# Fixed buffer places, a new order, x by token half and one scale per weight tile in a fused attention and MoE kernel

## The chip, the cores and the metric

One core of one Trainium2 chip runs the whole program; the other cores do nothing. The metric is the time of one execution on the device in microseconds, the median of several runs. Lower is better.

## What is computed

Three stages follow each other: a linear attention with decay in blocks of 64 rows, a gated layer without a nonlinearity, and a layer with a SoLU, a layer norm and an output projection.

```python
for b in range(nb):                       # q, k, v: (2, 8, 768, 64)
    intra = einsum('bhic,bhjc->bhij', qb, kb) * Dmask
    intra = einsum('bhij,bhjd->bhid', intra, vb)
    inter = einsum('bhid,bhde->bhie', qb * lam_pow, kv_state)
    out[:, :, sl] = intra + inter
    kv_state = lam_block * kv_state + einsum('bhsd,bhse->bhde', kb * rev_pow, vb)
x = out.transpose(0, 2, 1, 3).reshape(1536, 512)
x = ((x @ w_a) * (x @ w_b)) @ w_out       # 512 -> 1536 -> 512
h = x @ w_in                              # 512 -> 1024
solu = h * softmax(h)
ln = (solu - mean(solu)) / sqrt(var(solu) + 1e-6) * g_ln
return ln @ w_out2                        # 1024 -> 512
```

All inputs are float32.

## The kernel before

Every large product is done with numbers split into two float16 parts, high and low: `mm3` (line 142) issues three products for each one, high by high, high by low, low by high. The splitting is done on ScalarE (ACT, the high part), VectorE (DVE, the low part, by a SCALAR_TENSOR_TENSOR) and GpSimd (POOL). Before a split, a scale that is a power of two is found from the largest absolute value (`amax`, line 114, then `pow2`, line 128, which uses products on PE with the result `pm` to spread the value over the partitions).

The work is cut into 12 row tiles of 128 tokens for the attention (`n`), three token blocks of 512 (`t`), and weight tiles. Pieces of work are generators; each `next` issues one step. The letters in `ORDER` name them: G loads, A scores (`pss`, then `sc` on DVE), K and Q decays on POOL (`kd`, `qd`), C the attention's products (`px`) and their maximum `xst`, T the state (`pst`), X the scale of x (`sx`), Y its split (`xh`), J sums of x (`tt`, `xt`), D decodes a weight tile (`fab` and the like, and its maximum `st_ab`), p and P find the scale of weights (`sab`), S splits them (`wab`, `wo`, `wi`), H and E make sums of weights and split them (`s`, `ws`), L products of the gated layer in the plain way (`pa`, `pb`), R the same for a pair of weight tiles by seven instead of eight products with sums of halves (Strassen's way; `rA`, `rB`, `rC`, with `p` and `c` on ACT, DVE and POOL), M the projection back (`py`), U, V, B, F and the weight sums I, k the scale and the sums of y (`sy`, `yf`, `yu`, `yv`, `yt`), N the third layer's products (`hA`, `hB`, `hC`), n the SoLU and norm (`e`, `st`), Z the split and transposition of `e` (by DMA, and for the last two row tiles by PE: `pz`), W the output (`po`, `ob`).

`ORDER` is a long string of such words, written out. The engines run in the order in which it issues their instructions; nothing reorders them later. A word is one step, so the string is the whole schedule, for all engines and the DMA queue (SP) at once.

What the change and the prediction touch: tiles come from rotating pools, one each for `k` (41 buffers), `raw` (2), `row` (8), `state` (4) and the 8 PSUM banks (`bank`, line 103; `tile_of`, line 106), so a new tile takes the next buffer in turn. x is kept as two tiles by halves of the 512 model columns, each with all 512 tokens (`split_x`, line 290). Each row tile of 128 tokens has its own scale, two in one `sx` (line 286), and each weight tile has two, one for w_a and one for w_b, in `sab` (`scale_f`, `scale_w`, lines 358 and 361); so a split of a weight tile is two ACT and two DVE instructions of 512 or 256 columns (`split_w`, line 409; `split_s`, line 451). Products that compute nothing are issued by `warm` (line 182), with the identity as weights: 22 at the start, and by the table `FILL` 24 ahead of C 1, 36 ahead of T 5, 34 ahead of the scale X 3 and 18 ahead of C 8. `L1` (line 473) is the plain product, with 512 columns, except for block 0 and tile 0 (`HALVED`), where it is done by two halves of the tokens.

Of the kernel before, what the change touches and what calls it, by code (L numbers as in the profile page):

```python
# [86 lines left out]
PLAIN, PLAINW = [0, 1, 2], [0, 1]  # L87

TOP = 12
BUFS = {"k": 41, "raw": 2, "row": 8}  # L90
# [825 lines left out]
```

## Time and profile before

| | us |
|---|---|
| runs (3): lowest, median, highest | 455.75, 456.03, 456.63 |
| profiled execution: span, from its first to its last instruction | 454.0 |
| PE busy | 441.3 |
| DVE busy | 337.8 |
| ACT busy | 248.7 |
| POOL busy | 233.1 |

The span is that of one execution under the hardware profiler, and the page gives no time of its own for it beyond the span. The timed runs include what lies around the span; their median is 2.0 us above it. Busy times of an engine are merged, so that instructions that overlap are not counted twice.

### The profile page before, as it was taken

What the parts mean: (1) busy time and instruction counts of PE and PEld (TensorE: products, weight loads), DVE (VectorE), ACT (ScalarE), POOL (GpSimd) and SP (SyncE); (2) the same over time, 40 slices, a digit from 0 to 9 for tenths busy, and PEclk for the clock granted to TensorE, in tenths of its full rate; (3) what the DMA queues carried; (4) which work ended last, traced back from release to release, by engine and by line L of the source; (5) the groups of instructions that cost most, each with busy time, mean ns of one, the idle gap of its engine ahead of it and who ended that gap; (6) DMA issues with size and microseconds to landing.
All of it is one profiled execution on the core that took longest, in us unless ns stands there. A gap on an engine that the chain in (4) does not pass through costs nothing.

```text
span 454.0 us, 8039 instructions
## 1 busy us (share of the span) xinstructions
PE 441.3 (97%) x3204; PEld 276.5 (61%) x3204; DVE 337.8 (74%) x571; ACT 248.7 (55%) x397; POOL 233.1 (51%) x259
## 2 busy tenths in 40 slices
...
GB/s 302 415 214 270 196 92 281 185 186 95 94 0 1 2 1 165 121 180 0 95 92 76 203 99 88 0 95 1 1 20 39 60 23 95 68 116 90 144 47 46
DMA packets 30373, 48.76 MB, mean 107 GB/s; under 512 B 22272, under 2 KB 22528, under 8 KB 27008
## 3 DMA queue, kind: packets, MB, share of 16 engines
...
q14 instruction: 12, 0.10, 0.1%
...
## 4 chain that ended last, share of the span: by engine, by line
PE 74%; DVE 6%; POOL 4%; DMA 2%; ACT 1%; issue 1%; ACTq 0%; DVEq 0%; POOLq 0%
PE py L145 21%; PE rA L145 14%; PE po L145 13%; PE rB L145 7%; PE hA L145 4%; PE rC L145 3%; PE pa L145 3%; PE pb L145 3%; PE hB L145 2%; DMA raw<-in_wab_dram 2%; PE hC L145 1%; DVE fab L353 1%; DVE tt L320 1%; DVE ws L459 1%; DMA zT<-zr 1%
## 5 line engine op out<-in xcount | busy, mean ns | idle before, releaser
L145 PE MATMUL py<-g,wo 128*128 128x512 f16 x432 | 94.4, 379 | 0.0
L145 PEld LDWEIGHTS <-wab 128*128 128x128 f16 x744 | 72.1, 98 | 36.0 <-issue 0.9
L145 PEld LDWEIGHTS <-wo 128*128 128x128 f16 x432 | 42.2, 98 | 50.4
L145 PE MATMUL po<-wo,zT 128*128 128x512 f16 (+1 forms) x312 | 63.5, 363 | 0.3 <-DMA zT<-zr 0.3
L145 PEld LDWEIGHTS <-ws 128*128 128x128 f16 x576 | 56.1, 98 | 7.6 <-DVE ws L459 0.5
L145 PEld LDWEIGHTS <-zT 128*128 128x128 f16 x312 | 30.5, 98 | 32.0 <-DMA zT<-zr 0.8
L563 POOL TENSOR_TENSOR g<-c,g 128x512 f16<-128x512 f32 x24 | 31.2, 1319 | 33.8 <-ACT g L561 33.7
L145 PE MATMUL rA<-xt,ws 128*128 128x256 f16 x288 | 35.2, 273 | 0.0
L496 POOL TENSOR_TENSOR g<-asb,g 128x512 f16<-128x512 f32 x12 | 16.0, 1338 | 34.1 <-ACT g L494 34.1
L145 PE MATMUL pa<-xh,wab 128*128 128x512 f16 (+1 forms) x156 | 33.3, 363 | 0.0
L145 PE MATMUL pb<-xh,wab 128*128 128x512 f16 (+1 forms) x156 | 33.2, 363 | 0.0
L519 ACT ACTIVATE p<-rA 128x512 f32<-128x512 f32 x36 | 21.2, 595 | 20.5 <-PE rA L145 20.5
L807 POOL TENSOR_TENSOR zr<-e,zr 128x512 f16<-128x512 f32 x20 | 24.7, 1256 | 10.1 <-ACT zr L803 10.1
L351 ACT ACTIVATE raw<-raw 128x1024 f32<-128x1024 f32 x26 | 29.4, 1140 | 0.0
L848 ACT ACTIVATE ob<-po,glm 128x512 f32<-128x512 f32 (+1 forms) x13 | 8.4, 654 | 34.4 <-PE po L145 28.6
L552 POOL TENSOR_TENSOR c<-p,p 128x512 f32<-128x512 f32 x12 | 15.7, 1311 | 20.6 <-ACT p L519 19.6
L145 PEld LDWEIGHTS <-yt 128*128 128x128 f16 x144 | 14.0, 98 | 16.8 <-DVE yt L651 0.3
L557 DVE SCALAR_TENSOR_TENSOR c<-c 128x512 f32<-128x512 f32 x24 | 20.2, 850 | 4.9 <-ACT c L554 4.6
L425 ACT ACTIVATE wab<-fab,sab 128x512 f16<-128x512 f32 (+1 forms) x24 | 14.4, 641 | 10.5 <-DVE sab L136 10.4
L353 DVE SCALAR_TENSOR_TENSOR fab<-raw,fab 128x1024 uint32<-128x1024 uint32 x12 | 15.5, 1289 | 6.3 <-ACT raw L351 6.3
L764 ACT ACTIVATE e<-h,st,ch 128x512 f32<-128x512 f32 (+1 forms) x12 | 12.3, 1022 | 14.1 <-DVE st L758 14.1
L428 DVE SCALAR_TENSOR_TENSOR wab<-fab,sab,wab 128x512 f16<-128x512 f32 (+1 forms) x24 | 18.9, 822 | 1.1 <-ACT wab L425 1.1
...
## 6 DMA issues: line engine op xcount, KB each, us to landing
...
zT<-zr SPq DMA_TRANSPOSE x20, 3.1
...
```

The lines of the kernel that those rows point to most:

```text
L145: nc.tensor.matmul(o, w[a], x[b], start=start and i == 0, stop=stop and i == 2, skip_group_check=True)
L351: nc.scalar.activation(hi.bitcast(F32), hi.bitcast(F32), AF.Prelu, scale=2.0 ** -112, alpha=2.0 ** 32)
L353: nc.vector.scalar_tensor_tensor(out=flat, in0=hi, scalar=3, in1=flat, op0=ALU.logical_shift_left, op1=ALU.bitwise_or)
L425: nc.scalar.activation(w[:, z, 0, c], src[:, z, c], AF.Copy, scale=ss[:, z:z + 1])
L428: nc.vector.scalar_tensor_tensor(out=w[:, z, 1, c], in0=src[:, z, c], scalar=ss[:, z:z + 1], in1=w[:, z, 0, c], op0=ALU.mult, op1=ALU.subt ...
L496: nc.gpsimd.tensor_sub(g[:, 1], a, g[:, 0])
L519: nc.scalar.activation(r, o, AF.Copy, scale=2.0 ** -28)
L552: nc.gpsimd.tensor_sub(c1[:, 1], p167, p5)
L557: nc.vector.scalar_tensor_tensor(out=c[:, :, 0], in0=c[:, :, 0], scalar=2.0, in1=c[:, :, 1], op0=ALU.mult, op1=ALU.mult)
L563: nc.gpsimd.tensor_sub(g[:, 1], c[:, :, 0], g[:, 0])
L764: nc.scalar.activation(e2[:, z], x, AF.Exp, bias=st[:, 2:3], scale=c, accum_out=st[:, 3 + k:4 + k])
L807: nc.gpsimd.tensor_sub(lo, e[z], hi)
```

## The change

Five things change. `SLOTS` names for each new tile which buffer it takes, and the pools of small tiles give each its own place. `ORDER` is another string. x is kept as two tiles by token half, each with all 512 columns: one ACT and one DVE instruction of 512 columns split a row tile, where there were two each of 256, and two row tiles share one scale. L reads the two token halves apart, so its products have 256 columns, and those of block 0 and tile 0 have 128. A weight tile has one scale for w_a and w_b: its split, and that of its sums, is one ACT and one DVE instruction of twice the columns. `FILL` is empty; the products that compute nothing now have a tile of ones as weights that DVE writes at the very start, and a new word `w` issues four of them, 12 times in `ORDER`.

```diff
-FILL = {('C', 1): 24, ('T', 5): 36, ('X', 3): 34, ('C', 8): 18}
+FILL = {}
...
-         "A,1 D,ab,0 A,1 K,1 K,1 C,1 D,ab,0 Q,2 A,2 C,1 G,ab,2 G,qk,6 K,2 G,kv,6 C,2 A,2 Q,3 A,2 A,3 D,ab,0 X,0 C,2 K,3 A,3 K,3 T,1 X,0 K,2 p,0 A,3 T,1 C,3 O,3 "
...
+ORDER = ("G,qk,0 G,qk,2 G,qk,1 G,kv,0 G,kv,1 G,qk,3 w,9 G,qk,5 w,7 w,6 G,ab,0 G,kv,2 A,0 G,kv,3 A,2 Q,2 A,0 A,0 G,qk,4 A,1 A,2 A,1 G,kv,5 C,0 K,0 A,1 K,0 C,0 "
...
-BUFS = {"k": 41, "raw": 2, "row": 8}
...
+    "raw": ("01010101010101011010011010"),
...
+    "state": ("012301302130201320"),
...
+    taken = {tag: iter(SLOTS.get(tag, "")) for tag in ("bank", "k", "raw", "row", "state")}
+
+    def slot(tag):
+        return tag + str(ABC.index(next(taken[tag], "0")))
 
     def bank(nm):
-        return ps.tile([P, W], F32, tag="bank", name=nm)
+        return ps.tile([P, W], F32, tag=slot("bank"), name=nm)
...
-        nc.vector.tensor_reduce(out=m, in_=pm[:, :n * P].rearrange("p (g c) -> p g c", g=n), axis=AX.X, op=ALU.max)
+        nc.vector.tensor_reduce(out=m, in_=pm[:, :n * P], axis=AX.X, op=ALU.max)
...
+    hot = const.tile([P, P], BF16, name="hot")
+    nc.vector.memset(hot, 1.0)
...
-            nc.tensor.matmul(o, identb, identb, start=True, stop=True, skip_group_check=True)
+            nc.tensor.matmul(o, hot, hot, start=True, stop=True, skip_group_check=True)
+
+    def heat(i):
+        warm(bank("heat")[:, :P], 4)
+        yield
...
-            xs[t] = [t_k("xh", (P, 2, 2, W), F16) for _ in range(2)]
-        s = sx[n // 2][:, 0, n % 2:n % 2 + 1]
+            xs[t] = [t_k("xh", (P, KD, 2, W // 2), F16) for _ in range(2)]
+        s = sx[n // 2][:, 0]
...
-        for h in hs:
-            nc.scalar.activation(xs[t][h][:, :, 0, c], o[:, 2 * h:2 * h + 2], AF.Copy, scale=s)
-        yield
-        for h in hs:
-            xh, xl = (xs[t][h][:, :, z, c] for z in range(2))
-            nc.vector.scalar_tensor_tensor(out=xl, in0=o[:, 2 * h:2 * h + 2], scalar=s, in1=xh, op0=ALU.mult, op1=ALU.subtract)
+        xh, xl = (xs[t][j % 2][:, :, z, j // 2 * P:(j // 2 + 1) * P] for z in range(2))
+        nc.scalar.activation(xh, o, AF.Copy, scale=s)
+        yield
+        nc.vector.scalar_tensor_tensor(out=xl, in0=o, scalar=s, in1=xh, op0=ALU.mult, op1=ALU.subtract)
         yield
...
-        return pow2(stab[:, f // 2, f % 2], 2, sab[:, :, f], TOP)
+        return pow2(stab[:, f:f + 1], 1, sab[:, :, f:f + 1], TOP)
...
+    def both(hi, lo, src, s):
+
+        nc.scalar.activation(hi, src, AF.Copy, scale=s)
+        yield
+        nc.vector.scalar_tensor_tensor(out=lo, in0=src, scalar=s, in1=hi, op0=ALU.mult, op1=ALU.subtract)
         yield
...
+        if nm == "ab":
+            at = f if f // 2 in PLAINW else f - f % 2
+            c = slice(W // 2 if f % 2 and f // 2 not in PLAINW else 0, W)
+            yield from both(w[:, :, 0, c], w[:, :, 1, c], src[:, :, c], sab[:, 0, at:at + 1])
+            return
...
-        ss = sab[:, 0, 2 * p]
-        for z in range(2):
-            nc.scalar.activation(w[:, z, 0], src[:, z], AF.Copy, scale=ss[:, z:z + 1])
-            yield
...
+        yield from both(w[:, :, 0], w[:, :, 1], src, sab[:, 0, 2 * p:2 * p + 1])
...
-                    xk = x[kk // 2][:, kk % 2]
-                    mm3(rows(pp[z]), (w[:, 0, ks], w[:, 1, ks]), (rows(xk[:, 0]), rows(xk[:, 1])), kk == 0, kk == KD - 1)
+                    for q in range(2):
+                        xk = x[q][:, kk].rearrange("p z (i c) -> p z i c", i=2)[:, :, i]
+                        mm3(rows(pp[z])[:, q], (w[:, 0, ks], w[:, 1, ks]), (xk[:, 0], xk[:, 1]), q == 0 and kk == 0, q == 1 and kk == KD - 1)
```

The order on DVE at the start of the program, behind the decay masks. Before:

```order
L232 TENSOR_TENSOR sc<-pss,mask 128x512 x2
L115 TENSOR_REDUCE xst<-px 128x1
L232 TENSOR_TENSOR sc<-pss,mask 128x512 x2
L353 SCALAR_TENSOR_TENSOR fab<-raw,fab 128x1024
L115 TENSOR_REDUCE xst<-px 128x1
L232 TENSOR_TENSOR sc<-pss,mask 128x512 x2
```

With the change:

```order
L251 TENSOR_TENSOR sc<-pss,mask 128x512 x5
L128 TENSOR_REDUCE xst_221<-px 128x1 x2
L251 TENSOR_TENSOR sc<-pss,mask 128x512 x2
L146 TENSOR_REDUCE pm<-pm 128x1
L148 TENSOR_SCALAR pm<-pm 128x1
L149 TENSOR_SCALAR sx_256<-pm 128x1
```

The scores of two and a half row tiles come ahead of the first maximum of x, and the first scale of x ahead of the first decoded weight tile.

The order on DVE at the end of the program. `e` and `st` are the norm's tiles of the last two row tiles, `zT` their transposed parts. Before:

```order
L775 SCALAR_TENSOR_TENSOR e<-e,st,hA 128x512
L775 SCALAR_TENSOR_TENSOR e<-e,st,h_4633 128x512
L792 TENSOR_SCALAR e<-e,st 128x1024
L778 BN_STATS bn<-e 128x6 x2
L780 BN_AGGR st<-bn 128x2
L792 TENSOR_SCALAR e<-e,st 128x512 x2
L827 TENSOR_TENSOR zT<-pz,zT 128x4x128 x4
```

With the change:

```order
L794 BN_STATS bn_4877<-e 128x6 x2
L796 BN_AGGR st_4820<-bn_4877 128x2
L794 BN_STATS bn_4841<-e 128x6 x2
L808 TENSOR_SCALAR e<-e,st_4820 128x512
L796 BN_AGGR st_4825<-bn_4841 128x2
L808 TENSOR_SCALAR e<-e,st_4820 128x512
L808 TENSOR_SCALAR e<-e,st_4825 128x1024
L841 TENSOR_TENSOR zT<-pz,zT 128x4x128 x4
```

The row tile whose half lies in PSUM is now finished first, the other one (1024 columns) last, and the low parts of `zT` for both stand behind that.

On PE the transposes of the two row tiles stand together with the change, ahead of the first half of the last output tile:

```order
L158 LDWEIGHTS zT
L158 MATMUL po<-wo_3856,zT 128x512
L834 MATMUL pz<-ident,e 128x128 x16
L158 LDWEIGHTS zT
L158 MATMUL po<-wo_3647,zT 128x256
```

Before they were two groups of 8 with a whole output tile between them and one behind the second.

## Rows read from the trace of the kernel before

**Rows 1.** The page's busy times: share of the span, number of instructions.
```profile
PE 441.3 (97%) x3204; PEld 276.5 (61%) x3204; DVE 337.8 (74%) x571; ACT 248.7 (55%) x397; POOL 233.1 (51%) x259
```
**Rows 2.** Windows: stretch, length, then busy PE, PEld, DVE, ACT, POOL, clock, DMA share.
```profile
0.00:6.79 6.79, 4.61 (x38) 4.05 (x38) 3.08 (x9) 1.49 (x2) 3.94 (x16) 1.00 0.67 230
6.79:15.00 8.21, 7.91 (x104) 6.85 (x104) 4.94 (x7) 2.57 (x3) 3.77 (x6) 1.00 1.02 411
15.00:58.33 43.33, 37.43 (x598) 32.88 (x598) 37.79 (x80) 23.55 (x41) 33.29 (x38) 1.00 0.63 252
58.33:102.20 43.87, 43.19 (x282) 22.66 (x279) 40.41 (x62) 26.20 (x41) 24.89 (x19) 1.00 0.53 193
102.20:440.00 337.80, 337.50 (x2114) 203.07 (x2115) 250.29 (x415) 192.12 (x307) 167.20 (x184) 1.00 0.24 70
...
60.07:450.71 390.64, 390.09 (x2451) 231.84 (x2450) 290.25 (x475) 220.60 (x350) 190.64 (x200) 1.00 0.27 84
```
**Rows 3.** The chain of waits that ended last: start, us, what.
```profile
50.91 2.06 PE pm L184 x34
...
57.55 0.78 DVE xh L304 x2
...
60.07 2.69 PE pa L145 x12
...
66.38 1.02 PE px L249 x16
...
102.81 1.31 PE rA L145 x12
...
450.71 0.47 ACT ob L848
```
**Rows 4.** DVE's instructions by line and form: count, busy us, mean ns, idle before.
```profile
L428 DVE SCALAR_TENSOR_TENSOR wab<-fab,sab,wab 128x512 f16<-128x512 f32 x16 | 13.9, 904 | 1.1 <-ACT wab L425 1.1
L459 DVE SCALAR_TENSOR_TENSOR ws<-s,sab,ws 128x512 f16<-128x512 f32 x16 | 13.9, 917 | 0.0
L304 DVE SCALAR_TENSOR_TENSOR xh<-px,sx,xh 128x256 f16<-128x256 f32 x24 | 10.3, 475 | 1.1 <-ACT xh L300 0.9
L115 DVE TENSOR_REDUCE xst<-px 128x1 f32<-128x512 f32 x12 | 8.1, 685 | 3.9 <-PE px L249 3.9
L418 DVE SCALAR_TENSOR_TENSOR wo<-fo,s,wo 128x1024 f16<-128x1024 f32 x4 | 6.7, 1725 | 0.0
L679 DVE SCALAR_TENSOR_TENSOR wsi<-si,wsi 128x1024 f16<-128x1024 f32 x4 | 4.9, 1271 | 0.0
L775 DVE SCALAR_TENSOR_TENSOR e<-e,st,hA 128x512 f32<-128x512 f32 x6 | 4.5, 745 | 0.2
```
**Rows 5.** Timeline of the start: start, us, instructions, idle before and what ended it.
```profile
1.64 2.53 PE L184 MATMUL warm<-identb 128*128 128x128 bf16 x22 [1.64 <-DVE identb L179]
...
4.68 2.08 PE L227 MATMUL pss<-qk 64*128 64x128 f32 x16 [0.52 <-DMA qk<-in_qk_dram]
...
10.21 1.16 PE L227 MATMUL pss<-qk 64*128 64x128 f32 x16
```
**Rows 6.** Timeline around the scale of y for block 1.
```profile
299.10 0.22 PE L125 MATMUL pm<-identb,ry 128*128 128x128 bf16 x1
...
306.64 1.23 DVE L651 TENSOR_TENSOR yt<-yu,yt 128x1024 f16<-128x1024 f32 x1 [0.74 <-ACT yt L649]
```
**Rows 7.** Timeline of the end.
```profile
417.63 15.70 PE L145 MATMUL po<-wo,zT 128*128 128x512 f16 x72
...
431.93 1.00 DVE L792 TENSOR_SCALAR e<-e,st 128x512 f32<-128x512 f32 x2 [2.06 <-POOL st L789]
...
433.17 1.04 PE L820 MATMUL pz<-ident,e 128*128 128x128 f32 x8
```
**Rows 8.** DVE by line and form in 58.4:102.2 alone.
```profile
L459 DVE SCALAR_TENSOR_TENSOR ws<-s,sab,ws 128x512 f16<-128x512 f32 x3 | 4.9, 1679 | 0.0
...
L115 DVE TENSOR_REDUCE xst<-px 128x1 f32<-128x512 f32 x2 | 1.4, 692 | 0.6 <-PE px L249 0.6
```

More of the change, by code (lines that the diff above doesn't have):

```diff
@@ L89 @@
 TOP = 12
-BUFS = {"k": 41, "raw": 2, "row": 8}
+ABC = "0123456789abcdefghijklmnopqrstuvwxyzABCDEFGHIJKLMNOPQRSTUVWXYZ"
+SLOTS = {
+    "bank": ("01234567012345601475106140567056527053607563404761437653464636320621367013706123723076745367352137014670734161746713406225741236603623322603"
+          "0366143575102602364122012107635241064371206453"),
+    "k": ("0123456789abcdefghijklmnopqrstuvwxyzABCDE123ad4756cg98bkenphfmsoAtDqC2luBz3moy1bv9ebsuE60t24uzCs4581s41gAhgA60b51Evrflc01D6fDqB632qy7gD3yz8u"
+          "3y4zAnyuCdwapjixpjd29ouagwDismBeq06ktcwDjBfh6lpDfopjxfa3s0jprvyAafhn047bEksxCpmvl815zBjDAa6nrh04y"),
+    "raw": ("01010101010101011010011010"),
+    "row": ("012345671204576310241653025376134176704171701451047362264670232437402420232403701204127351246041652734102635407162342536720431256"),
+    "state": ("012301302130201320"),
+}
 @with_exitstack
@@ L251, in products @@
         if n // 2 not in xst:
-            xst[n // 2] = sm.tile([P, 2], F32, name="xst")
+            xst[n // 2] = sm.tile([P, 2], F32, name=f"xst{n // 2}")
         amax(xst[n // 2][:, n % 2:n % 2 + 1], o)
@@ L257, in fade @@
         b, c = order[n]
-        olds[n] = sl.tile([P, NP, D], F32, tag="state", name="old", bufs=4)
+        olds[n] = t_state("old", (P, NP, D))
         nc.gpsimd.tensor_mul(olds[n], state[n - B], dec[:, :, P - 1:P].to_broadcast([P, NP, D]))
@@ L271, in carry @@
         yield
-        new = sl.tile([P, NP, D], F32, tag="state", name="state", bufs=4)
+        new = t_state("state", (P, NP, D))
         if c == 0:
@@ L286, in scale_x @@
     def scale_x(m):
-        sx[m] = const.tile([P, 2, 2], F32, name=f"sx{m}")
-        return pow2(xst[m], 2, sx[m], TOP, FILL.get(("X", m), 0))
+        sx[m] = const.tile([P, 2, 1], F32, name=f"sx{m}")
+        yield from pow2(xst[m], 2, sx[m], TOP, FILL.get(("X", m), 0))
     def split_x(n):
@@ L334, in body @@
     wst = {nm: const.tile([P, m, 2], F32, name=f"st_{nm}") for nm, m in size.items() if nm != "ab"}
[L336 removed]
+    stab = const.tile([P, KA], F32, name="st_ab")
     fw, wt, scl = {}, {}, {}
[L339 removed]
+    sab = const.tile([P, 2, KA], F32, name="sab")
     def decode(nm, f):
         raw = raws.pop((nm, f))
[L344 removed]
+        hi = raw.rearrange("p z n w -> p (z n) w")[:, :, 1]
+        low = raw.rearrange("p z n w -> p (z n w)").bitcast(U16)[:, 1::4]
         x = fw[nm, f] = t_k("f" + nm, (P, 2, W))
         flat = x.rearrange("p z n -> p (z n)").bitcast(U32)
[L347 removed]
+        nc.scalar.activation(flat, low, AF.Copy, bias=-0.49994, scale=2.0 ** -13)
         yield
[L350 removed]
         nc.scalar.activation(hi.bitcast(F32), hi.bitcast(F32), AF.Prelu, scale=2.0 ** -112, alpha=2.0 ** 32)
@@ L371, in scale_w @@
             nc.vector.tensor_mul(st, st, gl)
-        r = sm.tile([P, 1], F32, name="r1")
+        r = sm.tile([P, 1], F32, name=f"r1{nm}")
         amax(r, st)
@@ L388, in scale_w @@
             k = 2 * len(PLAINW)
-            both = sab[:, 0, k:].rearrange("p (f e) z -> p f e z", e=2)
-            nc.vector.tensor_copy(both[:, :, 1], both[:, :, 0])
+            pairs = sab[:, 0, k:].rearrange("p (f e) -> p f e", e=2)
+            nc.vector.tensor_copy(pairs[:, :, 1], pairs[:, :, 0])
             turn(sab)
@@ L400, in scale_w @@
         yield
-    def halve(f, s, t):
-        nc.scalar.activation(t[:, 0, :], f, AF.Copy, scale=s)
+    def both(hi, lo, src, s):
+        nc.scalar.activation(hi, src, AF.Copy, scale=s)
         yield
-        nc.vector.scalar_tensor_tensor(out=t[:, 1, :], in0=f, scalar=s, in1=t[:, 0, :], op0=ALU.mult, op1=ALU.subtract)
+        nc.vector.scalar_tensor_tensor(out=lo, in0=src, scalar=s, in1=hi, op0=ALU.mult, op1=ALU.subtract)
         yield
@@ L415, in split_w @@
             s = scl["ro"][:, 2 * f:2 * f + 1] if nm == "o" else scl[nm][:, 0]
-            nc.scalar.activation(w[:, :, 0], src, AF.Copy, scale=s)
-            yield
-            nc.vector.scalar_tensor_tensor(out=w[:, :, 1], in0=src, scalar=s, in1=w[:, :, 0], op0=ALU.mult, op1=ALU.subtract)
-            yield
+            yield from both(w[:, :, 0], w[:, :, 1], src, s)
             return
-        ss = sab[:, 0, f if f // 2 in PLAINW else f - f % 2] if nm == "ab" else (scl["ro"] if nm == "o" else scl["glm"])[:, 2 * f:2 * f + 2]
-        c = slice(W // 2 if nm == "ab" and f % 2 and f // 2 not in PLAINW else 0, W)
+        if nm == "ab":
+            at = f if f // 2 in PLAINW else f - f % 2
+            c = slice(W // 2 if f % 2 and f // 2 not in PLAINW else 0, W)
+            yield from both(w[:, :, 0, c], w[:, :, 1, c], src[:, :, c], sab[:, 0, at:at + 1])
+            return
+        ss = (scl["ro"] if nm == "o" else scl["glm"])[:, 2 * f:2 * f + 2]
         for z in range(2):
-            nc.scalar.activation(w[:, z, 0, c], src[:, z, c], AF.Copy, scale=ss[:, z:z + 1])
+            nc.scalar.activation(w[:, z, 0], src[:, z], AF.Copy, scale=ss[:, z:z + 1])
             yield
         for z in range(2):
-            nc.vector.scalar_tensor_tensor(out=w[:, z, 1, c], in0=src[:, z, c], scalar=ss[:, z:z + 1], in1=w[:, z, 0, c], op0=ALU.mult, op1=ALU.subtract)
+            nc.vector.scalar_tensor_tensor(out=w[:, z, 1], in0=src[:, z], scalar=ss[:, z:z + 1], in1=w[:, z, 0], op0=ALU.mult, op1=ALU.subtract)
             yield
@@ L453, in split_s @@
         w = wt["s", p, k] = t_k("ws", (P, 2, 2, W), F16)
-        ss = sab[:, 0, 2 * p]
-        for z in range(2):
-            nc.scalar.activation(w[:, z, 0], src[:, z], AF.Copy, scale=ss[:, z:z + 1])
-            yield
-        for z in range(2):
-            nc.vector.scalar_tensor_tensor(out=w[:, z, 1], in0=src[:, z], scalar=ss[:, z:z + 1], in1=w[:, z, 0], op0=ALU.mult, op1=ALU.subtract)
-            yield
+        yield from both(w[:, :, 0], w[:, :, 1], src, sab[:, 0, 2 * p:2 * p + 1])
     gs = {t: {} for t in range(NB)}
@@ L505, in R1, with product @@
         u, v = (lambda z, k=k: wt["s", p, k][:, z] for k in range(2))
-        def product(o, w, k, x, i, start, stop):
+        def product(o, w, k, x, start, stop):
             for z in range(2):
@@ L511, in product, with part, sums @@
                     ks = slice((2 * k + kk) * P, (2 * k + kk + 1) * P)
-                    mm3(o[:, z], (w(z)[:, 0, ks], w(z)[:, 1, ks]), (x[:, kk, 0, i * H:(i + 1) * H], x[:, kk, 1, i * H:(i + 1) * H]), start and z == 0 and kk == 0, stop and z == 1 and kk == 1)
+                    mm3(o[:, z], (w(z)[:, 0, ks], w(z)[:, 1, ks]), (x[:, kk, 0], x[:, kk, 1]), start and z == 0 and kk == 0, stop and z == 1 and kk == 1)
+        def part(k, i):
+            return x[i][:, 2 * k:2 * k + 2]
+        def sums(k, i):
+            return xt[t][k][..., i * H:(i + 1) * H]
         def acc(nm):
@@ L522, in R1 @@
         A, Bk = acc("rA"), acc("rB")
-        product(A, f, 0, x[0], 0, True, False)
+        product(A, f, 0, part(0, 0), True, False)
         yield
-        product(Bk, u, 0, xt[t][0], 0, True, False)
+        product(Bk, u, 0, sums(0, 0), True, False)
         yield
@@ L528, in R1 @@
         yield
-        product(A, u, 1, xt[t][0], 1, False, False)
+        product(A, u, 1, sums(0, 1), False, False)
         yield
@@ L532, in R1 @@
         yield
-        product(Bk, v, 1, x[1], 1, False, True)
+        product(Bk, v, 1, part(1, 1), False, True)
         yield
@@ L536, in R1 @@
         yield
-        product(A, v, 0, xt[t][1], 0, False, False)
+        product(A, v, 0, sums(1, 0), False, False)
         yield
@@ L542, in R1 @@
         C = acc("rC")
-        product(C, f, 1, x[1], 0, True, True)
+        product(C, f, 1, part(1, 0), True, True)
         yield
@@ L546, in R1 @@
         yield
-        product(A, h, 1, xt[t][1], 1, False, True)
+        product(A, h, 1, sums(1, 1), False, True)
         yield
@@ L570, in L2 @@
         if t not in yst:
-            yst[t] = sm.tile([P, KD], F32, name="ym")
+            yst[t] = sm.tile([P, KD], F32, name=f"ym{t}")
         o = pys[t, d] = bank(f"py{d}")
@@ L582, in scale_y @@
     def scale_y(t):
-        r = sm.tile([P, 1], F32, name="ry")
+        r = sm.tile([P, 1], F32, name=f"ry{t}")
         amax(r, yst[t])
@@ L591, in scale_y @@
             turn(sx[m])
-        c = sm.tile([P, 1], F32, name="c")
+        c = sm.tile([P, 1], F32, name=f"c{t}")
         nc.vector.tensor_scalar(c, s[:, 1], scl["oi"], None, op0=ALU.mult)
-        for j in range(NJ):
-            n = t * NJ + j
-            ch = scl["ch", t, j] = const.tile([P, 2], F32, name=f"ch{t}{j}")
-            ix = sx[n // 2][:, 1, n % 2:n % 2 + 1]
+        for i in range(NJ // 2):
+            ch = scl["ch", t, i] = const.tile([P, 2], F32, name=f"ch{t}{i}")
+            ix = sx[2 * t + i][:, 1]
             nc.vector.scalar_tensor_tensor(out=ch[:, 0:1], in0=ix, scalar=ix, in1=c, op0=ALU.mult, op1=ALU.mult)
@@ L734, in L3 @@
         product(A, y[1], at[1], si(3), False, True)
+        hs[t, 2 * i + 1] = [A]
         yield
@@ L740, in L3 @@
         nc.gpsimd.tensor_sub(r, p167, p5)
-        hs[t, 2 * i + 1] = (A, r)
+        hs[t, 2 * i + 1].append(r)
         yield
     def norm(t, j):
-        ch = scl["ch", t, j]
+        ch = scl["ch", t, j // 2]
         c, cn = ch[:, 0:1], ch[:, 1:2]
-        st = sm.tile([P, 16], F32, name="st")
+        st = sm.tile([P, 16], F32, name=f"st{t}{j}")
         h = hs[t, j]
```

45 lines of the change are left out of this document (18 added, 27 removed), and 98 rows, old and new, of the table ORDER.

## Prediction

> **What bounds the kernel now.** I read the page's busy times first: PE is busy 97% of the span [rows 1], so time can only come out of PE's work or its 12.7 us of idle. The windows, by stage, tell where that idle lies [rows 2]: from the start of L1(1,0) at 60.07 to the last product at 450.71 PE is busy 390.09 of 390.64 us. Before 60.07 it is busy 51.2 us (441.3 - 390.1), so 8.9 us are idle, and the last 3.29 us are the output's tail. The kernel has two stages: a first one in which PE waits for something, and a second in which PE runs without a break.
>
> What the first stage waits for: the chain goes from DVE to PE and back until `xh` of row tile 7 ends at 58.33 [rows 3]; with it and a few products L1(1,0) can start. DVE is busy 3.08 + 4.94 + 37.79 = 45.8 us of these 58.33 [rows 2], and idle 12.5: 3.7 us until its first `sc`, 3.3 until 15 us while the DMA engines run at a share of 1.02, 5.5 after that. So DVE, and early on the loads, set when L1(1,0) starts; PE sets the rest. PE does fill this stage with 112 products that compute nothing.
>
> **PE's own work.** A 128-column product costs 2.06/34 = 60.6 ns, a 256-column one 1.31/12 = 109.2, a 512-column one 2.59/12 = 215.8 [rows 3]. Removed: 112 fillers, -6.8 us. Added: 12 `heat` steps of 4, +2.9. L1 reads x in two halves: 264 products of 512 columns become 528 of 256 (+0.7), and the 48 of L1(0,0) become 96 of 128 columns (+0.6). The single scale for w_a and w_b drops 4 products of `pm`, -0.4. Sum -3.0 us. All fillers stand ahead of L1(1,0), where PE waits anyway, so they pay nothing by themselves. Behind that point the order moves one C step (2.04 us) forward and one T step (0.6) back, L1's halves cost +0.7 and two `pm` leave: **-1.0 us**.
>
> **Start of L1(1,0).** I count what DVE does before it, by the order, with rows for each [rows 4]. Before: 17 `sc`, 8 maxima, 3 decodes and 2 maxima of `fab`, 16 `tt`, 16 halves of `xh`, 2 of `wab` and small ones, 46.9 us by the rows; it was busy 42.7 without the mask, a ratio of 0.91, since neighbours overlap. After: 20 `sc`, 4 decodes, 8 `tt`, and `xh` as 8 pieces of 512 at 0.745 (the row with a PSUM input) in place of 16 at 0.475: 45.1, times 0.91 = 41.1 us. So -1.6 us of work.
>
> DVE's idle I set at 7.7 us against 12.5. Until the first `sc` 3.2: the warm-up products no longer wait 1.64 us for `identb` [rows 5], but qk still lands near 4.7, so only half of that comes through, PE being faster for the first scores (2.08 us cold, 1.16 later [rows 5]). Until 15 us 2.0: qk 0, 2 and 1 come first and the order has five `sc` in a row, where before DVE stood until `px`. After that 2.5: it has `sc` and `tt` to do where it waited for the x scale. The ends are 6 and 12.5 (nothing gained). DVE is then done at 41.1 + 3.1 + 7.7 = 51.9. PE has 43.6 us of work before L1(1,0), mostly from 4.7 us on, so it can be there by about 50. I take 53.0 for 60.07: **-7.1 us**; the ends are -9 and -2.9.
>
> **The R stretch.** Here the order asks more of DVE. Between `xh` of tile 7 and L1(2,1), which now comes early and needs `xh` of tile 11, DVE has 7 + 3 decodes, 8 maxima of `fab`, 16 `tt`, 6 wide and 2 half `wab`, 5 wide `ws`, 7 products of L1, and small ones. A wide `wab` or `ws` of 1024 takes the place of two of 512 (0.904 and 0.917). No row shows it: the nearest are `wsi` 1.271 and `wo` 1.725 [rows 4]; I take 1.57, since two halves lose one fixed part of about 0.24 (2 x 0.904 - 1.57). By rows that is 73.2 us, and in 58.33:102.20 DVE was busy 40.4 for 41.4 by rows, 0.976 [rows 2]: 71.4. With 1.5 us of idle DVE is ready at 51.9 + 71.4 + 1.5 = 124.8. PE has 69.0 us of products between L1(1,0) and L1(2,1), so it is there at 122.0. PE waits **+2.8 us**, spread over the `ws` and `wab` it needs. The ends are 0 (1.271) and +9, worked out under the rivals. Before, PE had 0.7 us of idle in that stretch [rows 2].
>
> **Middle.** From U's `pm` to the second product of N(1,1) PE now has 9.0 us of other work; the chain through `yf`, `yu` and `yt` took 299.10 to 307.87 = 8.8 before [rows 6]. That is no margin: **+0.4 us**, ends 0 and 2. Other weights, `g` and `wo` are ready with over 6 us to spare by the sums of each engine's work, so they cost nothing as long as PE is not ahead of these sums by that much.
>
> **Tail.** Before, the last product of N(2,1) ended at 417.63, and its first transposes came at 433.2, the others one output tile later [rows 7]. Now both pairs stand together behind three output tiles, 3 x 5.2 = 15.5 us later. Behind N(2,1) DVE must do for both row tiles: two sums and three maxima, the exp's small steps, three products by the scale, four statistics, three last scalings, by the rows 12.7 us; it waits for two exps (1.7 and 0.9) and twice for POOL's 2 us of root (2.06 shown [rows 7], less what DVE does meanwhile: 2.6 together). That is 17.9 us. The first pair of transposes (0.9) is cover: 17.9 - 15.5 - 0.9 = 1.5, and 0.5 more as DVE is still at the tile before: **+2.0 us**, ends 0 and 4. In exchange no tile stands between; the last tile is unchanged.
>
> **Sum.** -7.1 - 1.0 + 2.8 + 0.4 + 2.0 = -2.9 us against the profiled execution's span of 454.0: 451.1. The median of the runs is 456.0, 2.0 above the span (launch and end); the same 2.0 on top gives **453.1 us**, 0.6% less.
>
> **Rivals.** 0.2% of this kernel is 0.9 us; a measurement can't tell less from no change, so "same" is 455.1 to 456.9.
>
> *The waits don't come (0.18).* If wide pieces cost 1.271 as `wsi` does, DVE needs 68.2 us and PE never waits in the R stretch; with a tail of +0.5 the sum is -7.1 - 1.0 + 0.5 = -7.6: 448.4 us. For it: DVE has idle in almost all of the second stage (250 of 337.8 us busy [rows 2]). Against it: `wo` at 1.725, four times.
>
> *DVE becomes the bound (0.20), the slower side.* POOL's sums of weights run beside `ws`, and there a 512-wide `ws` took 1.679 in place of 0.917 [rows 8]. If the wide one stretches in full, 3.36 us, for three of the five `ws` that PE needs, that is 3 x 1.79 = +5.4: 458.5. For all five it is +9.0: 462.1. It decides from +2.9, an average `ws` above 2.15 us, on. For it: before, DVE was already 92% busy there (40.4 of 43.9 us [rows 2]) and PE hardly waited. Against it: fewer and wider instructions also meet POOL less often.
> The Trainium skill (SBUF — State Buffer, Who interferes with whom) says that a DVE instruction with two SBUF inputs and a GpSimd instruction that reads SBUF shut each other out for a whole instruction. By that rule a wide `ws` waits once, not twice: 1.271 + (1.679 - 0.745) = 2.2 us as an estimate from the rows, +3.2 in all, and the time would be 456.3, no change. The trace agrees in that `ws` stretches beside POOL's sums and `xst`, with one input in PSUM, does not [rows 4, 8].
>
> *The early idle stays (0.10).* If the loads and not the order hold DVE back, L1(1,0) starts at 57.2 and the R stretch and the tail still cost 5.8: -2.9 - 1.0 + 5.8 = +1.9, 457.9. For it: the DMA share of 1.02.
>
> *PE falls back to its lower clock (0.06).* The first warm products took 115 ns each [rows 5], 128 columns at 1.2 GHz; the granted clock in the rows stays at 1.00. Without the fillers PE has some 6.7 us of work in the 11 us ahead of L1(0,0). If that costs the higher clock, L1(0,0) takes 11.7 us for 5.8, L1(1,0) starts near 59, and the later DVE wait is covered: -1.1 - 1.0 + 2.4 = +0.3, 456.3. The Trainium skill (TensorE: Matmul & The Clock Gate, HAM oscillation) says that idle gaps of PE bring the clock down. No row here shows a fall after the start.
>
> **How the numbers follow.** The forecast has 0.46, with a range of its own of 451 to 455.5: 0.43 of that is faster, 0.03 same. With the first rival faster is 0.61. Same is 0.03, the clock 0.06 and 0.04 from the mild form of the DVE rival: 0.13. The rest, 0.16 and 0.10, is slower: 0.26. The range reaches from 448.0, which holds the first rival, to 459.5, which holds the `ws` case with three of five; outside lie all five and both ends together.
>
> **What would show it.** Right: L1(1,0) starts near 53; between it and L1(2,1) PE shows waits of 1 to 5 us in sum, released by DVE `ws`, `wab` or `xh`; behind the third-last output tile PE waits 1 to 4 us for DVE's last scaling `e`; wide `ws` near 1.6. PE has 244 more products, busy about 3 us less in work. Wrong: L1(1,0) after 57, or waits of PE above 6 us in the R stretch, or waits in places that none of these steps names, such as a PSUM bank that an engine frees late, since every buffer now has a fixed place.

## Result and profile after

The changed kernel takes **444.52 us** (median of 4 runs, 444.46 to 444.59), the kernel before 455.89 beside it (455.04 to 456.63): a ratio of 0.9755, 95% interval 0.974 to 0.977. The forecast was 453.1 with a range of 448.0 to 459.5. The side was right, the size was not: 11.4 us came, not 2.9, and the time lies outside the range. In the profiled execution the span fell from 454.0 to 442.7.

The page's busy times after, to be read against [rows 1]:

```profile
PE 436.8 (99%) x3448; PEld 297.7 (67%) x3448; DVE 323.3 (73%) x524; ACT 241.0 (54%) x365; POOL 236.2 (53%) x259
```

PE has 4.5 us less work (441.3 to 436.8) and its idle time fell from 12.7 us to 5.9. The windows tell where; columns as in [rows 2]: stretch, length, busy PE, PEld, DVE, ACT, POOL, clock, DMA share. Cut at the start of L1(1,0), which moved from 60.07 [rows 3] to 49.42:

```profile
0.00:49.42 49.42, 47.57 (x753) 41.39 (x754) 42.67 (x84) 22.79 (x31) 33.13 (x53) 1.00 0.95 373
49.42:117.58 68.16, 68.08 (x683) 59.58 (x683) 65.92 (x98) 55.95 (x73) 41.73 (x30) 1.00 0.45 164
...
49.42:439.39 389.97, 389.20 (x2697) 256.29 (x2696) 280.62 (x441) 217.80 (x335) 203.09 (x207) 1.00 0.25 78
```

Nearly all of the gain, 10.65 of 11.3 us, lies ahead of L1(1,0). There the work of PE fell by 3.7 us (51.23 to 47.57) and its idle time by 7.0 (8.84 to 1.85). Behind that point the kernel is 0.65 us shorter (393.93 to 393.28). The chain of waits (start, us, what) is less one-sided: it runs over the loads and POOL until 20.85, over PE to 60.0, over DVE from there to 82.1, and then over PE again, with the scale of y from 290 to 304 in between.

```profile
1.64 4.57 DMA qk<-in_qk_dram
6.22 12.58 DMA kv<-in_kv_dram
18.87 1.94 POOL kd L231 x2
...
27.85 1.45 PE pa L158 x24
...
47.38 1.02 PE px L262 x16
48.40 1.02 PE px L268 x16
49.42 2.73 PE pa L158 x24
...
80.24 1.21 DVE st_ab L128
82.10 0.69 PE pst L289 x16
...
118.86 2.62 PE pa L158 x24
```

Of all waits of PE in the span, grouped by place and releaser, five of 0.2 us or more are left (total, times, longest). None is in the R stretch and none in the tail, where the forecast had put 4.8 us:

```profile
PE warm L199 <- DVE hot L181: 1.0, 1, 1.0
PE hB L158 <- DVE yt L665: 0.6, 1, 0.6
PE pst L289 <- POOL kd L231: 0.3, 1, 0.3
PE pss L246 <- DMA qk<-in_qk_dram: 0.2, 1, 0.2
PE px L268 <- DVE sc L251: 0.2, 1, 0.2
```

By the windows PE is idle for 0.08 us between L1(1,0) and 117.58, all of it ahead of the `pst` at 82.10, which needed DVE's `asb`. So the two engines are level at that point, though no wait of size shows.

The wide pieces of DVE in the stretch from L1(1,0) to `xh` of tile 11, by line and form (count, busy us, mean ns), which answer to [rows 4, 8]:

```profile
L420 DVE SCALAR_TENSOR_TENSOR wab<-fab,sab,wab 128x1024 f16<-128x1024 f32 x6 | 9.6, 1601 | 0.0
L420 DVE SCALAR_TENSOR_TENSOR ws<-s,sab,ws 128x1024 f16<-128x1024 f32 x5 | 7.2, 1444 | 0.0
L318 DVE SCALAR_TENSOR_TENSOR xh<-px,sx,xh 128x512 f16<-128x512 f32 x5 | 3.6, 739 | 0.0
```

The means are about what I took, 1.57 for `wab` and `ws` and 0.745 for `xh`. But 1.57 is not the price of one piece: seven of the eleven wide ones took 1.27 to 1.30 us, as `wsi` did, and the others 1.52 to 2.30, beside instructions of POOL.

### The profile page after: what moved, and what is told of

Same layout as the page of the kernel before. It is cut to its first block, busy times and chain, and to the rows that moved or that the text cites. A ratio compares the mean times of both kernels' runs of the same rounds, so it can differ in the third digit from the quotient of the medians.

```text
span 442.7 us, 8451 instructions
## 1 busy us (share of the span) xinstructions
PE 436.8 (99%) x3448; PEld 297.7 (67%) x3448; DVE 323.3 (73%) x524; ACT 241.0 (54%) x365; POOL 236.2 (53%) x259
## 4 chain that ended last, share of the span: by engine, by line
PE 86%; DVE 5%; DMA 4%; POOL 2%; ACT 1%; issue 1%; SPq 0%; ACTq 0%
PE py L158 20%; PE rA L158 14%; PE po L158 13%; PE rB L158 7%; PE hA L158 6%; PE pb L158 5%; PE pa L158 4%; PE rC L158 4%; DMA kv<-in_kv_dram 3%; PE hB L158 3%; PE px L262 2%; PE px L268 2%; PE hC L158 2%; PE pss L246 2%; DMA qk<-in_qk_dram 1%; PE pst L289 1%
## 5 line engine op out<-in xcount | busy, mean ns | idle before, releaser
L158 PEld LDWEIGHTS <-wab 128*128 128x128 f16 x1056 | 98.7, 98 | 12.2 <-issue 0.5
L158 PE MATMUL py<-g,wo 128*128 128x512 f16 x432 | 96.3, 379 | 0.0
L567 POOL TENSOR_TENSOR c<-p,p 128x512 f32<-128x512 f32 x12 | 18.4, 1538 | 39.3 <-DVE wo L420 14.0
L158 PE MATMUL pb<-xh,wab 128*128 128x256 f16 (+1 forms) x312 | 33.6, 264 | 0.0
L158 PE MATMUL pa<-xh,wab 128*128 128x256 f16 (+1 forms) x312 | 33.5, 264 | 0.0
L808 DVE TENSOR_SCALAR e<-e,st 128x512 f32<-128x512 f32 (+1 forms) x18 | 14.8, 846 | 12.8 <-POOL st L805 12.7
L817 ACT CAST zr<-e 128x512 f16<-128x512 f32 x20 | 11.6, 616 | 22.6 <-DVE e L808 22.6
L367 DVE SCALAR_TENSOR_TENSOR fo<-raw,fo 128x1024 uint32<-128x1024 uint32 x10 | 14.4, 1435 | 11.1 <-ACT raw L365 8.1
L800 POOL TENSOR_SCALAR st<-st 128x1 f32<-128x1 f32 x12 | 3.2, 265 | 34.7 <-DVE st L796 24.5
L780 ACT ACTIVATE e<-h,st,ch 128x1024 f32<-128x1024 f32 (+1 forms) x12 | 12.3, 1023 | 14.4 <-DVE st L774 13.9
L862 ACT ACTIVATE ob<-po,glm 128x512 f32<-128x512 f32 (+1 forms) x13 | 8.5, 652 | 19.9 <-PE po L158 17.9
```

Source lines behind the costliest of these rows:

```text
L158: nc.tensor.matmul(o, w[a], x[b], start=start and i == 0, stop=stop and i == 2, skip_group_check=True)
L367: nc.vector.scalar_tensor_tensor(out=flat, in0=hi, scalar=3, in1=flat, op0=ALU.logical_shift_left, op1=ALU.bitwise_or)
L567: nc.gpsimd.tensor_sub(c1[:, 1], p167, p5)
L780: nc.scalar.activation(e2[:, z], x, AF.Exp, bias=st[:, 2:3], scale=c, accum_out=st[:, 3 + k:4 + k])
L817: nc.scalar.copy(rows[0][:, z * W:(z + 1) * W], e[z])
```

## Experiments

All times are medians; each run had the kernel before beside it on its chip, at 455.9 to 456.2 us. Three theories stand against each other for the start: PE's own work sets it, DVE sets it (the forecast), or the loads do.

### PE's work ahead of L1(1,0)

**Without the heat products** (no products in `heat`, its bank is still taken):

```diff
 def heat(i):
-    warm(bank("heat")[:, :P], 4)
+    bank("heat")
     yield
```

> The changed kernel without its 48 heat products; everything else stays. Theory A (PE sets the start: in the changed kernel PE has almost no wait before L1(1,0), so its own work decides when that starts): L1(1,0) starts 2 to 2.9 us earlier, near 46.5 to 47.3, and the time falls from 444.5 to 441.6 to 442.5. Theory B (DVE sets the start, as the prediction had it): L1(1,0) stays at 49.4, PE shows 2 to 3 us of waits before it, the time stays at 444.5. Theory C (the heat products hold the clock): the granted clock falls below 1.00 before L1(1,0) and the time rises by 2 us or more.

444.07 us (ratio 0.9747, 0.9716 to 0.9778), 0.45 less than the change, with intervals that overlap. L1(1,0) starts at 48.75 by the chain, 0.7 earlier, and L1(0,0) at 27.83 as before the edit. None of the theories gives this alone: 2.9 us of PE's work went and 0.7 came. PE's timeline of this run shows one part of what was paid back (start, us, instructions, idle before and what ended it):

```profile
1.04 2.53 PE L199 MATMUL warm<-hot 128*128 128x128 bf16 x22 [1.04 <-DVE hot L181]
4.65 5.48 PE L246 MATMUL pss<-qk 64*128 64x128 f32 x48 [1.08 <-DMA qk<-in_qk_dram]
```

The first 48 products of the scores took 5.48 / 48 = 114 ns each, the pace of the warm-up products (2.53 / 22 = 115) and near that of 1.2 GHz: with the old loads, below, 32 of them take 3.42 us, 107 ns each, while the granted clock reads 0.50. In the changed kernel the heat products stand in the wait for qk, and the first 32 took 82 ns and the next 16 took 73:

```profile
4.77 2.64 PE L246 MATMUL pss<-qk 64*128 64x128 f32 x32
7.62 1.16 PE L246 MATMUL pss<-qk 64*128 64x128 f32 x16 [0.21 <-DMA qk<-in_qk_dram]
```

**Only the first 12 heat products**, those ahead of the scores, tests that:

```diff
-    warm(bank("heat")[:, :P], 4)
+    warm(bank("heat")[:, :P], 4 if i in (9, 7, 6) else 0)
```

> The changed kernel with only its first 12 heat products (those at 3.4 to 4.7 us, while PE waits for qk) and without the other 36, 2.2 us of PE's work before L1(1,0). Without any, the first scores ran at 114 ns for a product of 128 columns, as at the lower clock, and PE lost some 3 us there. If that cold start is what took the gain of the first run: L1(1,0) at 47.3 to 48.3, time 442.3 to 443.5. If DVE's chain up to L1(0,0) took it: L1(0,0) still at 27.8, only the 2 heat steps behind it count, time 443.7 to 444.1. If the later heat products are needed for the clock: 445 or more.

443.82 us (0.9727, 0.9709 to 0.9746); L1(0,0) at 27.32, L1(1,0) at 48.24, 1.2 us earlier for 2.2 us of work removed. The first 32 scores took 74 ns each here, so the cold start is gone, but the time is only 0.25 us below the run without any heat products, which isn't clear of the noise. The cold start isn't all of it: something else comes level with PE. In that run DVE is busy 4.97, 4.96 and 4.96 us in the three stretches of 5 us from 15 to 30.

**The old fillers put back** into the changed kernel:

```diff
-FILL = {}
+FILL = {('C', 1): 24, ('T', 5): 36, ('X', 3): 34, ('C', 8): 18}
```

> The changed kernel with the 112 filling products of the kernel before put back at the same steps (C1, T5, X3, C8), 6.8 us of PE work ahead of L1(1,0). Theory A (PE sets the start): L1(1,0) at 55 to 56, time 450 to 451.3. Theory B (DVE sets it): the fillers stand where PE would wait, L1(1,0) at 49.4 to 50.5, time 444.5 to 445.5.

451.35 us (0.990, 0.9874 to 0.9927), 6.8 more than the change: the fillers' 6.8 us of work in full. The chain of this run:

```profile
55.68 2.73 PE pa L158 x24
```

**The fillers taken out of the kernel before:**

```diff
-FILL = {('C', 1): 24, ('T', 5): 36, ('X', 3): 34, ('C', 8): 18}
+FILL = {}
```

> The kernel before without its 112 filling products. The prediction's step (they stand where PE waits anyway and pay nothing): time 455 to 456.5, L1(1,0) near 60. Rival (they were on the path): 449 to 452, L1(1,0) at 53 to 56. Second rival (they hold the clock): granted clock below 1.00 before L1(1,0), time above 457.

456.88 us (1.0012, 0.9992 to 1.0032): no difference. In sum the fillers cost nothing in the old order, as predicted, but their work counts in full in the new one. The sum has two sides, though. PE now waits where two of the four groups stood (3.2 us for POOL's `kd`, 2.5 for `xst`), and the second rival's sign came too: the granted clock fell to 0.62 at 25 to 30 us and to 0.59 from 55 us on, behind 5 us in which PE was busy for 0.85:

```profile
50.00:55.00 5.00, 0.85 (x10) 0.42 (x9) 4.91 (x13) 3.56 (x6) 3.66 (x4) 0.85 0.08 30
55.00:61.50 6.50, 6.50 (x81) 5.77 (x82) 5.43 (x12) 2.66 (x6) 5.25 (x8) 0.59 0.02 4
```

There 16 products of `px` took 1.97 us, where they take 1.09 in the kernel before, and PE ran to L1(1,0) without a break. It came at 61.48, 1.4 us later than before, and PE's busy time ahead of it fell by 2.05 us (51.23 to 49.18), not by 6.8. So in the old order the fillers also held the clock; what they would cost at a clock that stays up, no run shows.

### DVE's work

**More of it at the start:** the maxima of `fab` 0 and 2 are taken twice.

```diff
-            amax(stab[:, f:f + 1], x.rearrange("p z n -> p (z n)"))
+            for _ in range(2 if f in (0, 2) else 1):
+                amax(stab[:, f:f + 1], x.rearrange("p z n -> p (z n)"))
```

> The changed kernel with the maxima of fab 0 and 2 each taken twice: 2.3 to 2.4 us more work of DVE, one piece ahead of L1(0,0) and one beside it, nothing else. If PE alone sets the start (its work there is without a break): 444.5 to 445, L1(1,0) at 49.4 to 49.8. If PE and DVE come out level there: 1.5 to 2.4 us more, 446 to 447, L1(1,0) at 51 to 51.8.

446.68 us (0.9787, 0.9769 to 0.9804), 2.2 more for 2.3 us of DVE's work; L1(1,0) at 51.79, and PE's longest new wait is one of 1.2 us for the maximum `st_ab`. With the run of the fillers this says that PE and DVE run level ahead of L1(1,0): more work for either shows in full, less work for PE alone in part. Less work for DVE alone was not tried.

**More of it in the R stretch:** the same edit with `(5, 6, 7, 8, 9)`.

> The changed kernel with the maxima of fab 5, 6, 7, 8 and 9 each taken twice: five times 1.13 to 1.21 us, some 5.8 us more work of DVE between L1(1,0) and L1(2,1), nothing else. If DVE is just ahead of PE there (1.1 us of lead at L1(2,1), 2.2 us of idle in the stretch): 2.5 to 4.7 us more, 447 to 449.2, with waits of PE for DVE between 60 and 130 us. If DVE has wide slack: 444.5 to 445.5. If DVE already binds: 450.

449.48 us (0.9852, 0.9833 to 0.9873), 5.0 more for 5.8 of work, a little above the case of a small lead. The longest new wait, 1.3 us, is that of `pst` for DVE's `asb`, the place where the two were level. The windows of this run show DVE full and PE with holes; in the changed kernel PE is busy 10.00 and 9.92 there:

```profile
70.00:80.00 10.00, 8.90 (x92) 7.57 (x90) 9.96 (x12) 7.64 (x9) 7.42 (x5) 1.00 0.67 243
80.00:90.00 10.00, 8.65 (x94) 7.22 (x93) 9.90 (x14) 7.84 (x12) 5.17 (x5) 1.00 0.44 156
```

**Halves again:** `wab` and `ws` cut in two on ScalarE and DVE, in the new order.

```diff
+        two = [0, 1] if cut else [slice(0, 2)]
+        for z in two:
+            nc.scalar.activation(hi[:, z], src[:, z], AF.Copy, scale=s)
...
+        for z in two:
+            nc.vector.scalar_tensor_tensor(out=lo[:, z], in0=src[:, z], scalar=s, in1=hi[:, z], op0=ALU.mult, op1=ALU.subtract)
```

> The changed kernel with its wide wab and ws cut into two halves again, on ScalarE and on DVE, in the same place of the order. By the rows DVE's work between L1(1,0) and the xh of tile 11 grows by about 6 x (2 x 0.904 - 1.60) + 5 x (2 x 0.917 - 1.44) = 3.2 us, and DVE was ready there 1.1 us ahead of PE. If that lead is all the slack there is: 446 to 447. If PE never depends on it (other slack, waits elsewhere covered): 444.3 to 445. If the merging is a main part of the gain: above 448.

447.21 us (0.9804, 0.9781 to 0.9827): 2.7 more. In the profile of this run PE waits for DVE in and just behind the R stretch, 1.1 us at `rC` and 0.4 at `pa`. L1(1,0) comes at 50.24, 0.8 later, but behind a wait for qk of 1.3 us, as in other profiles.

**More in the tail:** the statistics of row tile (2,2) are taken twice.

```diff
+        if (t, j) == (2, 2):
+            for z in range(2):
+                nc.vector.bn_stats(out=bn[:, z, :], in_=e[z])
         nc.vector.bn_aggr(out=st[:, 8:10], in_=bn)
```

> The changed kernel with the two statistics of the second-last row tile taken twice: two more DVE instructions of 0.64 us in the chain behind N(2,1). In the changed kernel that chain ends as the first transposes run and PE shows no wait. If it ends just in time (about 0.1 us of margin between the last scaling and the second tile's transposes): 1.0 to 1.3 us more, 445.5 to 445.8, with a wait of PE for DVE's e. If there is a wide margin, as it would be if the prediction's 17.9 us were far off: no change, 444.4 to 444.7.

446.09 us (0.9774, 0.9755 to 0.9793), 1.6 more, and a new wait of PE:

```profile
PE pz L837 <- DVE e L811: 1.1, 1, 1.1
```

0.4 us of the rest lies at the start of the profiled execution, where L1(1,0) came at 49.86.

### Order, loads, steps, places

**The change's steps in the order of before**, with rotating buffers and without fillers. Of the four words of each wide piece the first and third place stay:

```diff
-ORDER = ("G,qk,0 G,qk,2 G,qk,1 G,kv,0 G,kv,1 G,qk,3 w,9 ...
+ORDER = ("G,qk,0 G,kv,0 G,qk,1 G,ab,0 G,kv,1 G,qk,2 G,kv,2 ...
...
-        return ps.tile([P, W], F32, tag=slot("bank"), name=nm)
+        return ps.tile([P, W], F32, tag="bank", name=nm)
```

> The changed kernel's steps (wide wab and ws, x by token half, one scale for w_a and w_b, no fillers, early hot memset) in the order of the kernel before, with that kernel's rotating buffers. If the steps themselves bring the gain: 444 to 449. If the order brings it: 452 to 456, L1(1,0) at 57 to 60. The same order with the old steps is the run of the kernel before without fillers.

456.69 us (1.0015, 1.0003 to 1.0028), L1(1,0) at 59.94. The wide pieces, x by token half and the single scale bring nothing in the old order: 0.2 us below the kernel before without fillers. The granted clock falls in both, to 0.62 ahead of L1(1,0) here. In the new order the merging of `wab` and `ws` alone is worth 2.7.

**The new order with rotating buffers:**

```diff
-            return sl.tile(list(shape), dt, tag=slot(tag), name=nm, bufs=1)
+            return sl.tile(list(shape), dt, tag=tag, name=nm, bufs=BUFS[tag])
```

> The changed kernel's order with the kernel before's rotating buffers (8 banks, 41 large, 8 row, 4 state buffers, taken in turn) in place of a fixed place for each. If the fixed places are part of the gain (a buffer that comes up in turn is still in use and its writer waits): 447 to 455, with waits of PE for engines that free a bank. If they only name what the order would take anyway: 444 to 445.5.

445.39 us (0.9758, 0.9739 to 0.9777). Fixed places are worth 0.9 us at most, and the interval overlaps with the change's; 0.35 of it is a later L1(1,0) in the profiled execution (49.77), with a wait for qk of 1.1 us.

**The first twelve loads in the old sequence**, the rest of the order unchanged (the loads alone are shown here, without the words between them; the places in `k` follow):

```diff
-G,qk,0 G,qk,2 G,qk,1 G,kv,0 G,kv,1 G,qk,3 G,qk,5 G,ab,0 G,kv,2 G,kv,3 G,qk,4 G,kv,5
+G,qk,0 G,kv,0 G,qk,1 G,ab,0 G,kv,1 G,qk,2 G,kv,2 G,qk,3 G,kv,3 G,qk,4 G,qk,5 G,kv,5
```

> The changed kernel with its first twelve loads in the sequence of the kernel before (qk 0, kv 0, qk 1, ab 0, kv 1, qk 2, ...) in place of qk 0, 2, 1, kv 0, 1, ... ; nothing else moves. qk 2 then lands behind 3.5 MB in place of 1 MB, some 10 to 11 us instead of 6. If the sequence of the loads is a main part of the earlier start: 447 to 450, L1(1,0) at 52 to 55. If only the order of the work on PE and DVE counts and the loads have slack: 444.4 to 445.5.

453.33 us (0.9932, 0.9911 to 0.9952): 8.8 more, beyond all that was expected. PE's timeline and its window in this run:

```profile
13.32 3.42 PE L246 MATMUL pss<-qk 64*128 64x128 f32 x32 [6.83 <-DMA qk<-in_qk_dram]
```

```profile
10.00:15.00 5.00, 1.68 (x16) 1.68 (x18) 0.00 (x0) 0.00 (x0) 1.59 (x2) 0.50 1.02 419
```

qk 2 lands 9.75 us after its issue. In 1.60:13.30 the DMA engines move 351 GB/s, 4.1 MB, where qk 2 and all loads ahead of it are 3.7 MB: some of the loads issued behind it moved beside it. PE stands for 6.8 us, the granted clock falls to 0.50, 1.2 GHz, and DVE does nothing from 10 to 15. L1(1,0) comes at 57.69.

**The new sequence of loads in the kernel before** (its first nine loads; again the loads alone):

```diff
-G,qk,0 G,kv,0 G,qk,1 G,ab,0 G,kv,1 G,qk,2 G,kv,2 G,qk,3 G,kv,3
+G,qk,0 G,qk,2 G,qk,1 G,kv,0 G,kv,1 G,qk,3 G,ab,0 G,kv,2 G,kv,3
```

> The kernel before with its first nine loads in the sequence that the change has (qk 0, qk 2, qk 1, kv 0, kv 1, qk 3, ab 0, kv 2, kv 3); its fillers and the order of its work stay. If the sequence of the loads alone brings a good part of the 10.7 us: 447 to 453, L1(1,0) at 50 to 57. If loads and the order of the work have to fit each other (the old order takes the products of chunk 0, which need kv 0, straight after its scores): 455 to 458, L1(1,0) at 59 to 62.

459.32 us (1.0076, 1.005 to 1.0103): 3.4 more than the kernel before, L1(1,0) at 63.16. So in the old order the new sequence of loads has no worth by itself. Loads and order of work have to fit each other.

### Attempts at a faster version

**Cover for the wait of N(1,1):** the second step of M(2,0) ahead of N(1,1)'s second-block product, with 12 heat products.

```diff
-N,0,0 N,1,1 V,1,2
+N,0,0 M,2,0 N,1,1 V,1,2
...
-N,0,0 N,0,0 N,0,0 M,2,0 R,2,5
+N,0,0 N,0,0 N,0,0 R,2,5
```

> The changed kernel with only its first 12 heat products (443.8 measured for that alone) and with the second step of M(2,0), 2.6 us of products of y, moved ahead of the product of N(1,1) that waits 0.6 us for yt. If that wait is simply covered: 0.6 us less, 443.0 to 443.4. If the delay of N(1,1) costs it again at the next norm: 443.6 to 444.2.

445.63 us (0.9774, 0.9752 to 0.9796), 1.8 more than with the heat edit alone. The wait for `yt` is gone and a larger one has come, for ScalarE's copies of the partial sums:

```profile
PE hA L158 <- ACT p L720: 1.7, 2, 1.4
```

**qk 0 ahead of the constants**, with 12 heat products:

```diff
     nc.vector.memset(hot, 1.0)
+    load_qk(0)
     first = const.tile([P, H + NP + KB], F32, name="first")
...
```

> The changed kernel with its first 12 heat products alone and with the load of qk 0 ahead of that of the small constants, so that it is issued 0.45 us sooner. If the first load is what the early chain hangs on: 0.2 to 0.5 us less than with the heat edit alone, 443.3 to 443.6. If DVE, which is busy from 15 us on without a break, takes it back: no difference, 443.7 to 444.0.

445.36 us (0.978, 0.9749 to 0.9812), six runs from 444.12 to 448.92: no gain.

**The heat edit and the change side by side:**

> The changed kernel with its first 12 heat products alone, beside the changed kernel on the same chip. If the 0.7 us measured before are real: 443.5 to 444.1 here, 0.1 to 0.25% below the changed kernel in the same call. If they were noise: no difference.

> The changed kernel itself, on the same chip as the three others, as the mark for them: 444.3 to 444.8. If its early loads land as unevenly as in the profiles of the other runs (waits for qk of 0.2 to 1.3 us), single runs up to 446.

443.90 us (0.9736, 0.9716 to 0.9756) and 444.75 (0.9755, 0.9735 to 0.9775). 0.85 us less side by side and 0.7 by the earlier medians: 12 heat products have the lowest time here, by some 0.2%, with intervals that overlap. In the changed kernel's second profile L1(1,0) starts at 50.36 and the span is 443.7: the first loads land unevenly, which is worth about 1 us.

## Why the prediction was wrong

- **What bounds the kernel before:** right in sum. By the run without them the fillers paid nothing in the old order; I left out that they held the clock there.
- **Start of L1(1,0), -7.1: the term was mis-sized**, -10.65 measured. I had `xh` of tile 7 at 51.9 from 44.2 us of DVE's work and 7.7 of idle. By the window DVE was busy 42.67 of 49.42 us, so 1.5 less, and idle 6.75, 0.95 less. The 1.1 us that I put between `xh` of tile 7 and L1(1,0) didn't exist. These three make up the 3.6. DVE's timeline has the `xh` of tiles 5, 6 and 7 in a row, to 49.64, so L1(1,0) began 0.2 us before that of tile 7 was done:

```profile
47.53 2.11 DVE L318 SCALAR_TENSOR_TENSOR xh<-px,sx,xh 128x512 f16<-128x512 f32 x3
```

  With x by token half the first three products read only the half of tiles 4 and 6, so what set the start was PE's own last `px`, and DVE was in time by about a tenth of a microsecond (three products of 109 ns from 49.42 on end at 49.75).
- **"They pay nothing by themselves": the step that misled**, though no term of the sum was made of it. It was taken from the old order and used for the new. PE's work ahead of L1(1,0) is 47.57 us, not the 43.6 that I had (my own terms give 49.2: 51.2, less 3.0, of which 1.0 lies behind that point), and with so little idle left it is as long as DVE's chain. With the fillers in, the new order gives 451.35: more than half of the gain is lost. The removal and the order have to be counted together. PE's work in all fell by 4.5 us, not 3.0.
- **R stretch, +2.8: failed**, 0 measured. The sum by rows was good: 73.2 us foretold, and the rows of that stretch sum to 72.7. The factor was wrong. I multiplied by 0.976, the ratio of 58.33:102.20 before, where rows were means over the whole kernel while `ws` beside POOL was dearer [rows 8]. Its own rows sum to 45.2 us for the same 40.41 busy, 0.89. Busy were now 65.92 us, a ratio of 0.91, the one that I had found for the first stage. So DVE had `xh` of tile 11 at 117.58, 1.3 us ahead of PE's L1(2,1) at 118.86. The lead is thin, and at the `pst` of 82.10 there was none, as the runs with 3.2 and 5.8 us more work show.
- **Tail, +2.0: failed**, 0 measured. I had 17.9 us of chain behind N(2,1), from [rows 7] among others, against 16.4 of cover. The chain took 16.3: N(2,1)'s last product ends near 411.4 and DVE's last scaling at 427.71. DVE's timeline, with the idle time and its releaser in brackets:

```profile
424.59 0.49 DVE L808 TENSOR_SCALAR e<-e,st 128x512 f32<-128x512 f32 x1
426.90 0.81 DVE L808 TENSOR_SCALAR e<-e,st 128x1024 f32<-128x1024 f32 x1 [1.81 <-POOL st L805]
```

  The transposes, 16 in a row from PE's timeline, begin with the tile that is ready and reach the other as it is scaled. The mechanism was right, as the run with 1.3 us more shows. That the small steps of the two tiles overlap more than I allowed is how I read the 1.6 us between the sums; no run takes it apart.

```profile
426.94 1.92 PE L834 MATMUL pz<-ident,e 128*128 128x128 f32 x16
```

- **Middle, +0.4:** 0.6 measured, the wait for `yt` that [rows 6] let expect. **Around the span, +2.0:** 1.8.
- **Rivals.** *The waits don't come* was right on the R stretch and nearly on the tail, but carried the same -7.1. *DVE becomes the bound*: the mean of a wide `ws` was 1.44 us, below the 2.15 from which it decides. One of five met POOL at work, the others took 1.27 to 1.30; here are the two in the timelines of POOL and DVE:

```profile
74.26 2.04 POOL L505 TENSOR_TENSOR g<-asb,g 128x512 f16<-128x512 f32 x1
```

```profile
75.27 2.11 DVE L420 SCALAR_TENSOR_TENSOR ws<-s,sab,ws 128x1024 f16<-128x1024 f32 x1
```

  Each is some 0.85 us longer than its like (1.16 and 1.27). The Trainium skill (SBUF — State Buffer, Who interferes with whom) has a lock for a whole instruction, from which I estimated 2.2 us for each `ws` and 456.3 in all. The pair agrees with the rule; what failed is that all five would meet POOL. *The early idle stays*: it takes the old sequence of loads, as the 453.3 show (its 5.8 us of later waits should have been 5.2 by the terms of the sum). *PE falls to its lower clock*: not in the change, whose granted clock reads 1.00 in every window up to the last product. It fell in the new order with the old loads and in the old order without fillers. The Trainium skill (TensorE: Matmul & The Clock Gate, HAM oscillation) says that idle gaps of PE bring the clock down. The 0.50 behind the 6.8 us of idle with the old loads agrees.

The three terms that failed have one sign: each rests on a sum of DVE's steps that came out too long, and two waits were put on the path for lags of 2 to 3 us in sums of 18 and 73.

What stays open: how the 9.7 us between the kernel before without fillers (456.9) and the new order with halves (447.2) divide. The latter also holds x by token half, the single scale, fixed places, and the heat products. The two runs that swap the loads alone both lose, so no sum of parts can be given.
